# Top-k attention and two feed-forward layers on one core: the steps behind one top-k pair moved up, two weight rows converted at the start

## The chip, the cores and the metric

The program runs on one core of one Trainium2 chip. The metric is the device time of one execution in microseconds (us). The kernel before took 1209.21 us (median of 3 runs, 1208.96 to 1211.28).

## What is computed

The reference, cut to its core:

```python
scores = scale * np.matmul(q, k.transpose(0, 1, 3, 2))      # 4 x 8 heads, 576 x 576, head size 64
kth = np.partition(scores, -top_k, axis=-1)[..., -top_k:-top_k + 1]   # top_k = 32
scores = np.where(scores >= kth, scores, -1000000000.0)
attn = np.exp(scores - np.max(scores, axis=-1, keepdims=True))
attn = attn / (np.sum(attn, axis=-1, keepdims=True) + 1e-09)
x = np.matmul(attn, v)                                      # as 2304 rows of 512
h = np.maximum(x @ w_in, 0.0);  x = h * h @ w_out           # first layer, 512 -> 2048 -> 512
h = x @ w_in;  out = np.maximum(0.01 * h, h) @ w_out        # second layer
```

## The kernel before, in words

**Attention.** 2304 query rows are cut into units (`UNITS`), each unit into four head pairs ("uh" in the code), each of these into tiles of 128 partitions x 576 scores; two neighbouring tiles are a *pair*, and there are 72. For a pair VectorE (DVE) finds the 32 largest of every row: four times MAX8 and three times MATCH_REPLACE8 per tile (L829, L831), 14 instructions, one per slot. The program is written as a list of events by *slot*, 16 slots to a pair. Behind the top-k of pair p (z = 16 p) stand: `shifts` on POOL (L288, L289), `drop` and `expo_sum` on ACT (L295, L299), `recip` on POOL and DVE (L303, L304), the transposes on TensorE and their copies on ACT (`pt_main`, `pt_left`, L313 to L362), the product with V on TensorE (`av`, L397), and `x_out`: a multiplication on DVE (tile `xn`, L428), a copy on ACT (`xh`, L429) and a difference on POOL (`xl`, L432). They were put at z + 14 to z + 34.

**Scores.** Tiles of batches 0 and 1 are scored just ahead of their top-k (tiles `sd`, later `att`, into buffers `s`). Those of batches 2 and 3 are scored early, spread over slots 2 to 245 (`FILL`): TensorE into `sp`, ACT into `stage` (L277), a DMA into DRAM (L280).

**The two layers.** Rows are gathered into blocks (`BLOCKS`, the first has 512 rows). When a block's last `x_out` is emitted, both layers of it start (`moe`): for each of 16 weight rows of a layer 12 matmuls into `h` (L575) and as many into `acc` (L618, L620), cut into quanta that are spread evenly over the slots up to the next block's completion (`rate`). The first block is complete with pair 15. At that slot (`rslot[0]`, 274) the pools of the early scores are closed and those of the layers opened, so `h` also waits for the last `sp` and `stage`.

**Weights.** A weight row comes from DRAM as two tiles `wraw` of 64-bit numbers (L486, 0.5 MB each; four buffers). `w_convert_steps` makes fp32 of each half and splits it: two ACTIVATEs (L509 into `wc`, L510 into a PSUM bank `att`), two SCALAR_TENSOR_TENSORs on DVE (L514, L515), an ACTIVATE (L519) and a POOL difference (L521) into `wi` or `wo`; it is then stored (L529, L530) for later blocks. Row 0 was loaded from slot `rslot[0]` - 80 on and converted at - 28, row 1 at - 14.

**What sets the order.** The Tile framework schedules the recorded instructions on each engine's in-order queue. `tc.high_priority(offset=...)` moves what is recorded inside it that many places forward in its ranking: events have `SOON = 100`, weight conversions `CONVP = 30` beside it.

```python
for fn, a in events.pop(slot, []):
    nr = len(ready)
    with tc.high_priority(offset=SOON):
        fn(*a)
```

Of the kernel before, what the change touches and what calls it, by code (L numbers as in the profile page):

```python
# [31 lines left out]
BLOCKS = [512, 256, 384, 512, 256, 384]  # L32
# [24 lines left out]
DLEAD = 30  # L57
LEAD = 24

SOON = 100  # L60
CONVP = 30

HI_SET = (0, 1, 2, 3, 4, 5, 6, 7, 8, 9, 10, 11, 12, 13, 14, 15)
# [8 lines left out]
def topk_attention_moe_moe2_kernel(  # L72
# [10 lines left out]
    B, NHP, _, _, S = q.shape  # L83
    D = v.shape[-1]
    P = 128
# [37 lines left out]
    uhs = []  # L123
    tiles = []
    for u in units:
        for hp in range(NHP):
            n = u["n"]
            uh = dict(u=u, hp=hp, n=n, b=u["b"], first=(u["t0"] == 0), ti=len(tiles), idx=len(uhs),
                      c0=P * (hp % 2) if n == 64 else 0)
# [14 lines left out]
    def direct(uh):  # L144
        return uh["b"] not in EARLY
# [4 lines left out]
    def split(uh):  # L150
        return uh["u"]["i"] >= NATIVE
# [35 lines left out]

    def at(slot, fn, *a):
        events.setdefault(slot, []).append((fn, a))


    KT = {}
# [299 lines left out]
    def w_convert(i):  # L492
        g = w_convert_steps(i)
        while True:
            with tc.high_priority(offset=CONVP):
                if next(g, 1):
# [150 lines left out]
    def score_slot(ti):  # L647
        return 16 * (ti // 2) - DLEAD + 5 * (ti % 2)
# [5 lines left out]
    for uh in uhs:  # L654
        b, hp, i = uh["b"], uh["hp"], uh.get("di")
        z = score_slot(uh["ti"])
        if uh["first"] and direct(uh):
            st = {"i": i}
            st["n"] = len(order)
            order.append(b)  # L660
            z0 = after(z - 62, ("kraw", st["n"] - KRB), *[("KT", x, hp) for x in range(b)])
            at(z0, load_k, b, hp, st)
            for h in range(2):
                at(z0 + 12 * h + 11, split_k, b, hp, st, h)
            used["kraw", st["n"]] = z0 + 23
            assert z0 + 24 <= z
        if (b, hp) not in vdone or split(uh) and VTB < NHP:
            assert not uh["u"]["i"] < NATIVE <= units[max(x["i"] for x in units if x["b"] == b)]["i"]
            vdone.add((b, hp))
            zv = z + DLEAD + 4  # L670
            if split(uh):
                zv = max(zv, opened)
            at(zv, load_v, uh)
            if split(uh):
                at(zv + 6, split_v, uh, 0)
                at(zv + 9, split_v, uh, 1)
# [55 lines left out]
        done += w  # L732

    pairs = []
    for p in range(NPAIRS):
        pr = dict(t=tiles[2 * p:2 * p + 2], p=p)
        pairs.append(pr)
        z = 16 * p
        for i, t in enumerate(pr["t"]):
            if direct(t["uh"]):  # L740
                at(z - DLEAD + 5 * i, scores, t, 0)
                at(z - DLEAD + 2 + 5 * i, scores, t, 1)
            else:
                at(z - LEAD + i, load_s, t)
            if i == 0:
                at(z + 14, shifts, pr)
            at(z + 14 + i, drop, pr, i)
            at(z + 16 + i, expo_sum, pr, i)
            if split(t["uh"]):
                at(z + 20 + i, norm, pr, i)  # L750
            at(max(z + 20 + 3 * i, z + 21 + i), pt_main, t)
        at(z + 18, recip, pr)
        at(z + 26, pt_left, pr)
    rslot = [None] * len(blocks)

    def rmark(uh, z):
        if uh["hp"] == NHP - 1:
            e = uh["u"]["g0"] + uh["n"]
            for blk in blocks:
                if rslot[blk["idx"]] is None and blk["g0"] + blk["n"] <= e:  # L760
                    rslot[blk["idx"]] = z

    for uh in uhs:
        if split(uh):
            za, z = 16 * (uh["lastA"] // 2) + 30, 16 * (uh["last"] // 2) + 30
            at(za, av_split, uh, 0)
            at(z + 2, av_split, uh, 1)
            z += 4
            at(z, x_out, uh, (0, 1))
            rmark(uh, z)  # L770
            continue
        apart = uh["n"] > P and uh["n"] % P and uh["ti"] % 2 == 0
        for hs in ((0,), (1,)) if apart else ((0, 1),):
            z = 16 * (uh["lastA"] // 2 if hs == (0,) else uh["last"] // 2) + 30
            nq = 2 * len(hs)
            for i in range(nq):
                at(z + i, av, uh, hs, i)
            at(z + nq, x_out, uh, hs)
        z += nq
        if uh["u"]["i"] == NATIVE - 1 and uh["hp"] == NHP - 1:  # L780
            at(z, open_late)
        rmark(uh, z)
# [6 lines left out]
        for _ in w_convert(i):  # L789
            pass  # L790

    at(rslot[0] - 80, w_raw, 0)
    at(rslot[0] - 80, w_raw, 1)
    at(rslot[0] - 28, convert_now, 0)
    at(rslot[0] - 27, w_raw, 2)
    at(rslot[0] - 14, convert_now, 1)
    at(rslot[0] - 13, w_raw, 3)
    at(rslot[0] - 10, w_store, 0)

    active = []  # L800
    credit = 0.0
# [11 lines left out]
    last = max(events)  # L813
    while slot <= last:
        p, i = divmod(slot, 16)
        if slot >= 0 and p < NPAIRS:
            pr = pairs[p]
# [7 lines left out]
            t = pr["t"][x]  # L825
# [9 lines left out]
# [4 lines that stand above are left out]
# [66 lines left out]
```

## Time and profile before

| | us |
|---|---|
| median of 3 runs (1208.96 to 1211.28) | 1209.21 |
| the profiled execution | 1210.15 |
| its span, first to last instruction | 1208.4 |
| TensorE (PE) busy | 1135.8 (94%) |
| VectorE (DVE) busy | 946.5 (78%) |
| ScalarE (ACT) busy | 807.5 (67%) |
| GpSimd (POOL) busy | 682.8 (57%) |

The profile shows one execution; a time in it is counted from the span's first instruction. An instruction's row gives its start, its length, engine, line, operation and `output<-input`; brackets give the idle time of the engine before it and what ended it. Instructions of one engine overlap a little, so what one costs in a full queue is the distance of two starts. PE's busy time is modelled, and a PE that is busy is not always at its peak. The chain of waits is followed back from the last instruction: at each step to what released it, or to the instruction ahead of it on its engine.

### The profile page before, as it was taken

The page shows a single profiled execution, that of the slowest core. Times are in us where ns is not written, and L with a number is a line of the kernel's source. Part 1 is how long each engine was busy: PE and PEld are TensorE (multiplying, and loading weights), DVE is VectorE, ACT ScalarE, POOL GpSimd, SP SyncE. Part 2 cuts the span into 40 slices and gives each one's busy share as a digit, 9 for nine tenths or more (in the row PEclk, how much of TensorE's full clock was granted, in tenths as well). Part 3 has the DMA queues.
Part 4 walks back from the last instruction along what each step waited for, and adds up shares of the span by engine and source line. Part 5 has one row for each costly group of instructions (what it writes and reads, how often), then busy time and mean ns, then how long its engine had stood idle before and what let it go on. Part 6 is the DMA issues. An engine that isn't in the chain of part 4 may idle for free.

```text
span 1208.4 us, 20261 instructions
## 1 busy us (share of the span) xinstructions
PE 1135.8 (94%) x6388; PEld 992.5 (82%) x6388; DVE 946.5 (78%) x1944; ACT 807.5 (67%) x1831; POOL 682.8 (57%) x982
## 2 busy tenths in 40 slices
PE   4988987999889999999999999999999999999998
PEld 3776765887678779988999898888788899999997
DVE  7999899868988999999999999999999930110122
ACT  6988898878998986766656666555666653334322
POOL 7765564877878876556666665555565644004300
PEclk9899897999999999999999999999999999999999
DMA  9765566779989888879988888776676679779974
GB/s 307 255 217 192 192 220 222 267 233 333 342 280 319 305 267 263 296 269 384 355 293 290 298 272 286 221 227 226 201 239 211 199 255 369 253 253 341 356 256 135
DMA packets 110522, 323.25 MB, mean 268 GB/s; under 512 B 17488, under 2 KB 25680, under 8 KB 110416
## 3 DMA queue, kind: packets, MB, share of 16 engines
q1 hardware_dynamic: 107776, 317.24, 77.5%
q10 hardware_dynamic: 2640, 4.72, 1.1%
q8 instruction: 52, 0.85, 0.3%
q14 instruction: 54, 0.44, 0.1%
HBM read 254.54 MB, written 67.37 MB: 266 GB/s over the span
## 4 chain that ended last, share of the span: by engine, by line
PE 71%; ACT 11%; DVE 7%; DMA 6%; issue 2%; POOL 1%; ACTq 0%; SPq 0%; POOLq 0%; DVEq 0%
PE h L575 29%; PE acc L620 14%; PE acc L618 14%; PE att L408 4%; PE att L313 4%; DVE m L829 3%; PE att L397 3%; DVE w L831 3%; DMA wraw<-in_w_dram 2%; DMA sd<-stage 2%; ACT stage L277 1%; ACT e L299 1%; ACT e L295 1%; ACT s L277 1%; PE sp L276 1%
## 5 line engine op out<-in xcount | busy, mean ns | idle before, releaser
L575 PE MATMUL h<-xh,wi 128*128 128x512 f32 (+2 forms) x1280 | 349.9, 345 | 13.4 <-ACT gb L597 4.2
L829 DVE MAX8 m<-w 128x8 f32<-128x576 f32 x432 | 311.9, 748 | 1.1
L575 PEld LDWEIGHTS h<-xh,wi 128*128 128x128 f32 x1280 | 227.5, 191 | 42.6 <-ACT gb L597 5.8
L831 DVE MATCH_REPLACE8 w<-m,w 128x576 f32<-128x576 f32 x288 | 213.5, 744 | 0.8
L575 PE MATMUL h<-xl,wi 128*128 128x512 f32 (+2 forms) x640 | 207.6, 342 | 0.6 <-DVE xl L632 0.6
L601 POOL TENSOR_TENSOR gl<-ga,gh 128x512 fp32r<-128x512 f32 (+2 forms) x160 | 162.7, 1017 | 37.9 <-ACT gh L600 32.1
L618 PE MATMUL acc<-gh,wo 128*128 128x512 f32 (+2 forms) x768 | 156.8, 340 | 0.0
L620 PE MATMUL acc<-wo,gh 128*128 128x512 f32 x576 | 152.5, 399 | 2.9 <-ACT gh L600 2.7
L598 POOL TENSOR_TENSOR ga<-ga,gb 128x512 f32<-128x512 f32 (+2 forms) x80 | 81.4, 1017 | 130.6 <-ACT gb L597 127.3
L618 PEld LDWEIGHTS acc<-gh,wo 128*128 128x128 f32 x768 | 126.5, 189 | 11.0 <-ACT gh L586 0.2
L575 PEld LDWEIGHTS h<-xl,wi 128*128 128x128 f32 x640 | 121.4, 191 | 12.3 <-DVE xl L632 1.1
L295 ACT ACTIVATE e<-s,m 128x576 f32<-128x576 f32 x144 | 111.7, 779 | 18.6 <-DVE m L829 13.4
L620 PEld LDWEIGHTS acc<-wo,gh 128*128 128x128 f32 x576 | 104.3, 189 | 24.1 <-ACT gh L600 5.0
L829 DVE MAX8 m<-s 128x8 f32<-128x576 f32 x144 | 104.1, 748 | 12.5 <-ACT s L277 6.1
L299 ACT ACTIVATE e<-e,nb 128x576 f32<-128x576 f32 x144 | 111.0, 774 | 3.2 <-POOL nb L289 2.8
L587 POOL TENSOR_TENSOR ga<-ga 128x512 f32<-128x512 f32 (+2 forms) x80 | 66.1, 827 | 78.1 <-ACT gh L586 72.8
L831 DVE MATCH_REPLACE8 w<-m,s 128x576 f32<-128x576 f32 x144 | 107.1, 744 | 0.6
L313 PE MATMUL att<-ident,e 128*128 128x128 f32 x576 | 90.8, 281 | 13.7 <-ACT e L299 5.1
L313 PEld LDWEIGHTS att<-ident,e 128*128 128x128 f32 x576 | 70.0, 143 | 27.4 <-ACT e L299 10.1
L308 POOL TENSOR_SCALAR e<-e,rc 128x576 f32<-128x576 f32 x108 | 79.8, 749 | 22.5 <-DVE rc L304 21.1
L585 ACT ACTIVATE ga<-h 128x512 f32<-128x512 f32 (+2 forms) x80 | 39.0, 488 | 77.4 <-PE h L575 71.9
L618 PE MATMUL acc<-gl,wo 128*128 128x512 f32 (+2 forms) x384 | 87.7, 345 | 0.1
(94 smaller groups left out, 2136.7 us busy)
## 6 DMA issues: line engine op xcount, KB each, us to landing
wi<-wd SPq DMA_DIRECT2D x160, 512.0 KB, 5.0
wo<-wd SPq DMA_DIRECT2D x160, 512.0 KB, 5.2
wraw<-in_w_dram SPq DMA_DIRECT2D x64, 512.0 KB, 6.0
sd<-stage SPq DMA_DIRECT2D x72, 288.0 KB, 2.9
s<-sd SPq DMA_DIRECT2D x72, 288.0 KB, 4.6
wd<-wi SPq DMA_DIRECT2D x32, 512.0 KB, 5.4
wd<-wo SPq DMA_DIRECT2D x32, 512.0 KB, 5.9
kraw<-in_k_dram SPq DMA_DIRECT2D x16, 576.0 KB, 5.4
```

Source lines behind the costliest of these rows:

```text
L295: ACT.activation(t["e"], t["s"], AF.Prelu, bias=pr["m8"][:, i, 31:32], scale=-1.0, alpha=0.125 / FAR)
L299: ACT.activation(e, e, AF.Exp, bias=pr["nb"][:, i:i + 1], scale=-FAR, accum_out=pr["sum"][:, i:i + 1])
L308: POOL.tensor_scalar(e, e, pr["rc"][:, i:i + 1], 1.0, op0=OP.mult, op1=OP.mult)
L313: PE.transpose(ps[:, j * P:(j + 1) * P], t["e"][:, j * P:(j + 1) * P], ident)
L575: PE.matmul(h[:, 0:n], lhsT=wi[:, w, c * P:(c + 1) * P], rhs=x[c][y][:, 0:n], start=cnt == 0, stop=cnt == 3 * NK - 1)
L587: POOL.tensor_tensor(a[:, 0:n], a[:, 0:n], a[:, 0:n], op=OP.mult)
L598: POOL.tensor_tensor(a[:, 0:n], a[:, 0:n], b[:, 0:n], op=OP.subtract)
L601: (DVE if j >= GLD else POOL).tensor_tensor(gl[:, 0:n], a[:, 0:n], gh.bitcast(F)[:, 0:n], op=OP.subtract)
L618: PE.matmul(acc[c][:, 0:n], lhsT=wo[:, w, cs], rhs=g[:, 0:n], start=first, stop=last)
L620: PE.matmul(acc[c], lhsT=g[:, cs], rhs=wo[:, w, :], start=first, stop=last)
L829: cur["dve"] = DVE.max(out=m8[:, x, 8 * r:8 * r + 8], in_=t["s"] if r == 0 else t["w"])
L831: cur["dve"] = DVE.match_replace(out=t["w"], in_to_replace=m8[:, x, 8 * r:8 * r + 8], in_values=t["s"] if r == 0 else t["w"], imm_value=NEG)
```

## The change

Three edits go together. The steps behind pair 15's top-k are recorded at z + 13 and z + 14, with a priority of 800 places (`urgent`), and so are the second head's product with V and its `x_out`; for that head pair the two heads are now handled apart, the first at slot 251 and the second at 255. `rslot[0]` becomes 257 instead of 274, so the layers' quanta of the first block are spread over 176 slots instead of 159. Weight rows 0 and 1 are loaded at slots -20 and -19 and converted at -6 and -3, ahead of the first top-k, and rows 2 and 3 are loaded from `rslot[0]` - 60 on.

```diff
+URGENT = 800
...
+    def urgent(fn):
+        def run(*a):
+            with tc.high_priority(offset=URGENT):
+                fn(*a)
+        return run
...
+    first_done = next(uh["last"] // 2 for uh in uhs if uh["hp"] == NHP - 1 and uh["u"]["g0"] + uh["n"] >= BLOCKS[0])
...
+        if p == first_done:
...
+            at(z + 13, urgent(shifts), pr)
+            for i in range(2):
+                at(z + 13, urgent(drop), pr, i)
+                at(z + 13, urgent(expo_sum), pr, i)
+            at(z + 13, urgent(recip), pr)
+            for i in range(2):
+                at(z + 14, urgent(pt_main), pr["t"][i])
+            at(z + 14, urgent(pt_left), pr)
+            continue
...
-        apart = uh["n"] > P and uh["n"] % P and uh["ti"] % 2 == 0
+        tight = uh["last"] // 2 == first_done
+        apart = uh["n"] > P and (uh["n"] % P or tight) and uh["ti"] % 2 == 0
         for hs in ((0,), (1,)) if apart else ((0, 1),):
-            z = 16 * (uh["lastA"] // 2 if hs == (0,) else uh["last"] // 2) + 30
+            near = tight and hs[-1] == 1
+            z = 16 * (uh["lastA"] // 2 if hs == (0,) else uh["last"] // 2) + (15 if near else 27 if tight and apart else 30)
             nq = 2 * len(hs)
             for i in range(nq):
-                at(z + i, av, uh, hs, i)
-            at(z + nq, x_out, uh, hs)
+                at(z + i, urgent(av) if near else av, uh, hs, i)
+            at(z + nq, urgent(x_out) if near else x_out, uh, hs)
...
-    at(rslot[0] - 80, w_raw, 0)
-    at(rslot[0] - 80, w_raw, 1)
-    at(rslot[0] - 28, convert_now, 0)
-    at(rslot[0] - 27, w_raw, 2)
-    at(rslot[0] - 14, convert_now, 1)
-    at(rslot[0] - 13, w_raw, 3)
-    at(rslot[0] - 10, w_store, 0)
+    for i in range(2):
+        at(i - DLEAD + 10, w_raw, i)
+        at(3 * i - 6, convert_now, i)
+        at(rslot[0] - 60, w_raw, i + 2)
+    at(20, w_store, 0)
```

The order in which the built programs' instructions stand shows what the scheduler makes of it. Line numbers of the changed kernel are 7 higher up to L362, L397 becomes L404, L428 L435, L514 and L515 become L521 and L522, L829 and L831 become L851 and L853.

**DVE at the start.** Before; `m8` is the top-k's result, `s0` to `s3` are score buffers:

```order
1 L255 TENSOR_TENSOR q10_78<-qraw_148,q00_77 128x256 x2
2 L238 TENSOR_TENSOR KT_150<-kraw_151,KT_150 64x576 x2
3 L829 MAX m8_217<-s0_101 128x8
4 L831 MATCH_REPLACE w_220<-m8_217,s0_101 128x576
5 L829 MAX m8_217<-s1_102 128x8
6 L829 MAX m8_217<-w_220 128x8
7 L831 MATCH_REPLACE w_221<-m8_217,s1_102 128x576
```

The same place in the changed kernel:

```order
1 L262 TENSOR_TENSOR q10_78<-qraw_148,q00_77 128x256 x2
2 L521 SCALAR_TENSOR_TENSOR wc_223<-att_224,wc_223 128x512
3 L522 SCALAR_TENSOR_TENSOR wc_223<-att_224,wc_223 128x512
4 L245 TENSOR_TENSOR KT_150<-kraw_151,KT_150 64x576 x2
5 L521 SCALAR_TENSOR_TENSOR wc_231<-att_232,wc_231 128x512
6 L851 MAX m8_261<-s0_101 128x8
7 L522 SCALAR_TENSOR_TENSOR wc_231<-att_232,wc_231 128x512
8 L853 MATCH_REPLACE w_264<-m8_261,s0_101 128x576
9 L521 SCALAR_TENSOR_TENSOR wc_245<-att_246,wc_245 128x512
10 L851 MAX m8_261<-w_264 128x8
```

Three instructions of the conversion now stand ahead of the first MAX8, five more in rows 7 to 15; the same eight stood in rows 249 to 274 before.

**DVE between pair 15's last MAX8 and the first block's last `xn`**, in the changed kernel: `m8_2358` is pair 15, `m8_2499` pair 16, `m8_2729` pair 17.

```order
259 L851 MAX m8_2358<-w_2362 128x8
260 L851 MAX m8_2499<-w_2502 128x8
261 L853 MATCH_REPLACE w_2503<-m8_2499,w_2503 128x576
...
268 L853 MATCH_REPLACE w_2502<-m8_2499,w_2502 128x576
269 L435 TENSOR_TENSOR xn_2472<-att_2448,rb_2444 64x256
270 L851 MAX m8_2499<-w_2503 128x8
...
275 L521 SCALAR_TENSOR_TENSOR wc_2528<-att_2529,wc_2528 128x512
...
279 L853 MATCH_REPLACE w_2733<-m8_2729,s5_106 128x576
280 L435 TENSOR_TENSOR xn_2516<-att_2495,rb_2444 64x256
```

Before, pair 15's last MAX8 stands in row 254 and the last `xn` in row 288. In the changed kernel the distance is 21 rows instead of 34. Row 275 is the first on weight row 2 (`wc_2528`), ahead of the last `xn`; before, that was row 290, behind it. Counted from the program's start, the last `xn` has 104 MATCH_REPLACEs, 139 MAXes, 10 SCALAR_TENSOR_TENSORs and one other `xn` of this head pair ahead of it, where there were 108, 145, 8 and none.

**ACT at the start**, in the changed kernel; before, row 2 was followed by the `KT` row at once:

```order
2 L114 ACTIVATE q00_77<-qraw_148 128x256 x2
3 L516 ACTIVATE wc_223<-wraw_191 128x512
4 L517 ACTIVATE att_224<-wraw_191 128x512
5 L114 ACTIVATE KT_150<-kraw_151 128x576 x2
6 L114 ACTIVATE q01_83<-qraw_157 128x256 x2
7 L526 ACTIVATE wi_221<-wc_223 128x512
8 L516 ACTIVATE wc_231<-wraw_193 128x512
9 L517 ACTIVATE att_232<-wraw_193 128x512
10 L284 ACTIVATE s0_101<-sd_179 128x288
11 L284 ACTIVATE s0_101<-sd_172 128x288
```

The eviction of the first scores (`s0`) now stands behind the conversion of the first two `wraw` tiles, and rows 12 to 17 alternate `s1` with the third and fourth.

## Rows read from the trace of the kernel before

**Rows 1.** Busy time by stage: window, length, PE, PEld, DVE, ACT, POOL, clock, DMA

```profile
0.00:204.00 204.00, 160.50 (x852) 128.19 (x853) 188.41 (x402) 174.81 (x461) 129.03 (x226) 0.92 0.70 230
204.00:444.00 240.00, 226.97 (x1109) 184.97 (x1107) 204.35 (x387) 210.59 (x436) 194.50 (x214) 0.99 0.85 292
```

**Rows 2.** Chain of waits by line, from 440 to 960 and from 960 us on

```profile
by line: PE h L575 36.2%; PE acc L620 18.0%; PE acc L618 17.1%; PE att L408 7.7%; PE att L313 6.2%; PE att L326 1.5%; DVE m L829 1.5%; PE att L276 1.3%; DVE w L831 1.3%; DVE xl L632 1.0%; POOL VT L230 0.8%; ACT y L635 0.7%; DMA wo<-wd 0.6%;
...
by line: PE h L575 46.1%; PE acc L620 24.4%; PE acc L618 22.9%; PE att L408 1.7%; ACT y L635 1.3%; PE att L313 1.0%; ACTq L637 0.4%; issue 0.3%; PE att L326 0.2%; ACT ga L585 0.2%; ACTq L635 0.0%
```

**Rows 3.** Timeline of PE where the first layer starts

```profile
203.68 1.43 PE L575 MATMUL h<-xh,wi 128*128 128x512 f32 x5 [0.87 <-ACT xh L429]
204.94 1.07 PE L575 MATMUL h<-xl,wi 128*128 128x512 f32 x4
```

**Rows 4.** Timelines of POOL, DVE and ACT: three steps behind pair 15's top-k

```profile
179.77 0.20 POOL L288 TENSOR_TENSOR nb<-m 128x2 f32<-128x2 f32 x1 [0.42 <-DVE m L829]
...
201.68 0.42 DVE L428 TENSOR_TENSOR xn<-att,rb 128x256 f32<-128x256 f32 x1
...
203.22 0.41 ACT L429 ACTIVATE xh<-xn 128x256 fp32r<-128x256 f32 x1
```

**Rows 5.** Timeline of DVE in a full queue: the distance between starts

```profile
188.87 0.67 DVE L514 SCALAR_TENSOR_TENSOR wc<-att,wc 128x512 uint32<-128x512 uint32 x1
189.45 0.08 DVE L831 MATCH_VALUE_LOAD w<-m,w 128x8 f32 x1
...
198.90 0.08 DVE L831 MATCH_VALUE_LOAD w<-m,w 128x8 f32 x1
...
199.63 1.41 DVE L829 MAX8 m<-w 128x8 f32<-128x576 f32 x2
```

**Rows 6.** Timeline of the start, and the busy time and DMA rate (GB/s, last) there

```profile
1.45 0.58 SPq L201 DMA_DIRECT2D kraw<-in_k_dram  x1
...
5.61 1.25 ACT L113 ACTIVATE KT<-kraw 128x576 fp32r<-128x576 f32 x2 [0.90 <-DMA kraw<-in_k_dram]
...
9.01 0.76 DVE L829 MAX8 m<-s 128x8 f32<-128x576 f32 x1 [1.25 <-ACT s L277]
...
12.11 1.30 POOL L115 TENSOR_SCALAR KTa<-kraw 128x576 fp32r<-128x576 f32 x2
...
0.00:10.00 10.00, 2.60 (x8) 1.96 (x8) 3.15 (x7) 5.09 (x10) 5.48 (x31) 1.00 0.77 261
...
20.00:30.00 10.00, 6.17 (x37) 4.68 (x35) 9.98 (x22) 9.27 (x24) 6.99 (x12) 1.00 1.03 382
```

**Rows 7.** What DVE waited for from 0 to 204 us: total, times, longest

```profile
DVE m L829 <- ACT e L295: 5.6, 4, 2.8
DVE q L255 <- ACT q L113: 4.4, 1, 4.4
```

**Rows 8.** The early scores' matmuls (min/median/max ns, first and last start), and the chain from 48 to 176 us

```profile
L276 PE MATMUL sp<-KTa,q x320: 288/295/609, 17.3 to 179.4; 128*128 128x288 f32 x160
...
by line: PE att L397 22.4%; DMA sd<-stage 14.3%; ACT stage L277 13.3%; PE sp L276 9.6%; ACT s L277 6.1%; issue 5.9%; PE sd L276 4.9%; ACT e L299 4.4%; PE att L313 4.1%; ACT PT L321 3.5%; ACT e L295 2.5%; ACT q L113 2.4%; ACT KT L113 1.8%; P
```

**Rows 9.** Chain from 204 to 444 us, and what DVE waited for there

```profile
by line: PE h L575 20.0%; DMA wraw<-in_w_dram 11.4%; PE acc L618 9.8%; PE acc L620 7.8%; issue 4.5%; DMA vraw<-in_v_dram 4.4%; ACT att L510 4.0%; ACT e L299 3.3%; ACT e L295 3.0%; ACT wc L509 2.9%; PE att L397 2.5%; PE att L313 2.1%; ACT gh
...
DVE wc L514 <- ACT att L510: 19.4, 14, 4.9
```

**Rows 10.** Timelines: an idle ACT queue, and DVE's first step on weight row 2

```profile
200.76 0.41 ACT L277 ACTIVATE s<-att 128x288 f32<-128x288 f32 x1 [2.77 <-PE att L276]
...
202.74 0.68 DVE L514 SCALAR_TENSOR_TENSOR wc<-att,wc 128x512 uint32<-128x512 uint32 x1
```

**Rows 11.** PE at low and at full clock: a window, and two stretches of `av`

```profile
180.00:200.00 20.00, 13.28 (x40) 9.19 (x41) 19.04 (x41) 16.38 (x37) 9.42 (x12) 0.57 0.75 264
...
193.79 6.67 PE L397 MATMUL att<-PT,VN 128*128 128x256 f32 x18
...
167.09 2.62 PE L397 MATMUL att<-PT,VN 128*128 128x256 f32 x10 [1.42 <-ACT PT L321]
```

More of the change, by code (lines that the diff above doesn't have):

```diff
@@ L738, in topk_attention_moe_moe2_kernel @@
         z = 16 * p
+        if p == first_done:
+            assert all(direct(t["uh"]) and not split(t["uh"]) for t in pr["t"])
+            for i, t in enumerate(pr["t"]):
+                at(z - DLEAD + 5 * i, scores, t, 0)
+                at(z - DLEAD + 2 + 5 * i, scores, t, 1)
+            at(z + 13, urgent(shifts), pr)
[7 more added lines that the diff above has]
+            continue
         for i, t in enumerate(pr["t"]):
```

## The prediction

> **What bounds the kernel now.** I read the busy time by stage first, then the chain of waits for each stage, then timelines where two stages meet. The busy table [rows 1] cuts the span in two at 204 us: the reader is to see that PE is idle for 204 - 160.5 = 43.5 us before the layers start, and for 240 - 227.0 = 13 us between 204 and 444 us. From 440 us on the chain [rows 2] is nearly all PE: `h`, `acc` and the attention's own matmuls follow each other, and DVE has under 4% of it up to 960 us and next to none behind. So what is worth anything is PE time lost before 444 us; behind that the end moves with it, one for one.
>
> The first block's layers start in earnest at 203.68 us, when the last `xh` lets five matmuls go, and the first on `xl` follows at 204.94 [rows 3]. What they wait for begins at 179.77, where POOL starts on the finished top-k of pair 15; the last `xn` comes at 201.68 and its `xh` at 203.22 [rows 4]. That is 21.9 us from top-k to `xn`, for a dozen instructions none of which takes 1 us: they stand behind others in in-order queues. The change aims there.
>
> **The change, part by part.** *The queue ahead of the last `xn`.* In a full DVE queue a MATCH_REPLACE8 with its load takes 199.63 - 198.90 = 0.73 us, a MAX8 1.41 / 2 = 0.70, a step of the conversion 189.45 - 188.87 = 0.58 [rows 5]. By the order, the last `xn` now has 4 MATCH_REPLACEs and 6 MAXes fewer ahead of it (2.9 + 4.2 us) and two conversion steps (1.2) and one `xn` (0.4) more: 5.5 us less. It is not the whole 21.9: 16 top-k instructions of the next two pairs, two conversion steps and another `xn` still stand between pair 15 and that `xn`, some 13 us, and the scheduler put them there because the chain through ACT, PE and back takes about as long. The other moved steps are the same instructions on the same engines; splitting one `x_out` in two adds one instruction of 0.42 us or so on each of DVE, ACT and POOL [rows 4], which lies beside other work.
>
> *The two weight rows at the start.* Moved are 8 DVE steps, 12 ACTIVATEs, 4 POOL differences, 4 loads and 4 stores. DVE's and ACT's share is already in the count above, since these stood ahead of the last `xn` before as well; they cost nothing unless DVE waits for them. The four loads do cost: each is 128 x 1024 x 4 bytes = 0.52 MB, the first now ahead of the first K (0.59 MB) on SP's queue, the others directly behind it and one q tile (0.26 MB). K was issued at 1.45 us and ACT had it at 5.61 [rows 6]. ACT now evicts the first scores only behind the second weight tile, which has 1.3 MB more ahead of it and in it than K had. At the 261 GB/s of the first 10 us or the 382 of the third 10 us [rows 6] that is 5.0 or 3.4 us, so it lands at 9.0 to 10.6; with two conversions at 0.62 (as K's halves) and two evictions at 0.41 [rows 6, 10] behind it, 2.0 us, the first MAX8 starts at 11.0 to 12.6 instead of 9.01. DVE fills 1.8 us of that with three conversion steps, so its idle time grows by 0.2 to 1.8, and perhaps by 1 more at the third and fourth tile. I take 1.3.
>
> The Trainium skill (DMA: Bandwidth & Descriptors, "Anatomy of one DMA") puts the moving of data at bytes / 436e9 s, by which the added 1.3 MB would take 3.0 us and the sum below would be about 1.5 us better. The trace's windows at 261 and 382 GB/s do not reach that rate, and they decide.
>
> *Sum for the layers' start.* DVE's other waits (5.6 us in four places behind ACT, rest at the start [rows 7]) I leave as they are. The last `xn`: 201.68 - 5.5 + 1.3 = 197.5, 4.2 earlier, and with it the first `h` on the last head pair, at 199.5. PE has then done 6 score matmuls and 4 transposes fewer; at half of 295 ns [rows 8] each, as they overlap, that is 1.5 us to be done later. PE idle time saved: 2.7 us.
>
> *The early scores* could be the next thing late: `h` waits for the last of them. Their K is loaded behind 2.1 MB more (5.5 to 8.0 us at the two rates), and two POOL differences now stand ahead of its split, priced at 1.30 us each by the longest POOL row near [rows 6]. So they start 8 to 11 us later than 17.3, at 25 to 28, and with the 162 us they took before [rows 8] the last comes at 188 to 190. That is covered by some 9 us; without the cover each us costs one.
>
> *The weights behind the start.* Between 204 and 444 us the chain leaves PE often: the loads of `wraw` have 11.4% of it, and DVE waited 19.4 us for conversions [rows 9]. DVE's first step on weight row 2 came 0.9 us ahead of the full `h` (202.74 against 203.68 [rows 3, 10]); now it stands five rows ahead of the last `xn`, 3.3 us by [rows 5], so 5.3 us ahead of `h`. This lead of 4.4 us is used once. If only PE binds it is worth 0, if the weights bind all of it. As the chain shows both, I take 2.5.
>
> *Sum.* 2.7 + 2.5 = 5.2 us: 1210.15 - 5.2 = 1205.0 for the profiled execution, which stood 0.94 above the median of the runs; for the median 1209.21 - 5.2 = **1204.0 us**. The forecast's own range is 1201 to 1206.5.
>
> **Rivals.** *DVE takes it back, no change (0.21).* The ten top-k instructions that no longer precede the last `xn` are still to be done, 5.5 us of DVE net, now between 204 and 444 us. DVE is idle for 240 - 204.4 = 35.6 us there [rows 1], which speaks against it; but 19.4 of that are waits inside its in-order queue [rows 9], which more work doesn't fill by itself. If none is filled, the block ends 5.5 later after a start 4.2 earlier: 1210.5.
>
> *The first stage is late as a whole, slower (0.13).* Place: the score evictions on ACT behind loads of weights, and the early scores' K. From 48 to 176 us the chain is made of `av`, `stage`, its DMA and `sp`, and DVE doesn't lead it [rows 8]; then the pace isn't DVE's, and the 8 to 11 us by which the early scores start late shift all of it, pair 15 too. The moved steps win 21.9 - 13 = 8.9 us at the most if every one goes at once; if half of it, `h` starts 9.5 - 4.5 = 5 us later. It decides from 204.6 us on for the first of the five matmuls (203.68, less the 1.5 us of PE work left over, plus 2.4); at 207 the time is 1209.2 + 3.3 + 1.5 = 1214. Against it: DVE is 188.4 of 204 us busy [rows 1].
>
> The Trainium skill (TensorE: Matmul & The Clock Gate, "Architectural detail") says that ACT and DVE are strict FIFO; by that rule a conversion that waits for its load holds every eviction behind it, which is this rival's mechanism. The trace agrees as far as it shows: ACT sat idle for 2.77 us at 200.76 behind one eviction [rows 10].
>
> *More than forecast (0.18).* PE ran at a granted clock of 0.57 from 180 to 200 us, mostly at its lower level of 1.2 GHz, after standing idle, and 18 matmuls of `av` took 6.67 us where 10 took 2.62 at full clock [rows 11]: 6.67 - 18 x 0.262 = 2.0 us on pair 15's path. With early scores now next to these steps PE need not fall to the lower level. If that, half of DVE's 5.6 us of waits [rows 7] and the whole 4.4 of the weights come: 2.7 + 2.0 + 2.8 + 4.4 = 11.9, so 1197.5 to 1201.
>
> *The change doesn't do what it says (0.02):* the order shows it does, though 16 top-k instructions remain between; the time would be 1209.
>
> **How the numbers follow.** Forecast 0.46, the others as given. A measurement of this kernel tells about 0.2% from no change, 2.4 us, so "faster" is below 1206.8. It holds the forecast save 0.02 and all of "more": 0.62. Slower, above 1211.6: the late stage, and 0.02 of the DVE case with a late start: 0.15. The rest is 0.23. The range reaches from 1198, which leaves out a small part of "more", to 1211.5, which leaves out the slower case.
>
> **What would show it.** Right: the first MAX8 at 11.0 to 12.6 us, the last `xn` near 197.5, the five matmuls of `h` near 199.5, the last `sp` near 190 and ahead of it, `h` and `acc` of the first block done some 5 us before 444, and the chain all PE behind that. Wrong: `h` held by `stage` or `sp` instead of `xh`; a first `h` near 199 with the first block's end unmoved, DVE busier between (the first rival); or PE stalls behind 444 us of more than the few it has, by the new order of its queue, which I can't price and take for 2 us either way.

## The result: slower by half a per cent, and the profile after

The changed kernel takes 1216.49 us (median of 17 runs, 1211.61 to 1225.25), the kernel before 1210.40 in the same job (17 runs, 1207.81 to 1212.95): a ratio of 1.0052, 95% interval 1.0039 to 1.0065. The forecast was 1204.0, faster. The profiled execution took 1212.28 us (span 1210.5), one of the fastest of its kernel, so its trace shows some 2 of the 6 us.

The busy time by stage of the changed kernel, and 740 to 760 us, where the difference lies; columns as in [rows 1]:

```profile
0.00:204.00 204.00, 158.58 (x847) 127.69 (x848) 186.46 (x397) 173.85 (x459) 131.00 (x227) 0.96 0.70 231
204.00:444.00 240.00, 226.49 (x1110) 182.78 (x1109) 203.65 (x388) 210.94 (x437) 192.28 (x212) 1.00 0.85 289
740.00:760.00 20.00, 14.34 (x60) 10.91 (x59) 19.77 (x42) 11.94 (x25) 4.68 (x11) 0.74 0.62 194
```

The last window in the kernel before:

```profile
740.00:760.00 20.00, 17.99 (x91) 14.45 (x90) 19.76 (x42) 13.48 (x29) 9.50 (x15) 1.00 0.81 271
```

The first two rows hardly differ from [rows 1]. In the third PE did 60 matmuls instead of 91, at a granted clock of 0.74 instead of 1.00, while DVE was busy for 19.8 of 20 us in both. Timelines of DVE, POOL, ACT and PE of the changed kernel, up to where the first layer starts (answering to [rows 3, 4, 6]); the POOL row is its first step on pair 15's top-k:

```profile
12.91 0.76 DVE L851 MAX8 m<-s 128x8 f32<-128x576 f32 x1
...
187.30 0.19 POOL L295 TENSOR_TENSOR nb<-m 128x2 f32<-128x2 f32 x1
...
198.84 0.43 DVE L435 TENSOR_TENSOR xn<-att,rb 64x256 f32<-64x256 f32 x1
...
202.25 0.41 ACT L436 ACTIVATE xh<-xn 64x256 fp32r<-64x256 f32 x1
...
199.65 0.96 PE L582 MATMUL h<-xh,wi 128*128 128x512 f32 x3 [0.84 <-ACT stage L284]
...
202.72 1.43 PE L582 MATMUL h<-xh,wi 128*128 128x512 f32 x5
203.99 1.09 PE L582 MATMUL h<-xl,wi 128*128 128x512 f32 x4
```

The layers start 1 us earlier, not 4. Still, PE gets ahead: the second layer's first outputs `y` (L642, before L635) of the first three blocks come at 445.3, 577.8 and 743.5 us, before at 445.9, 587.0 and 746.9. Part of the 9 us in the middle is order: by 578 us PE had done 2909 matmuls against 2889, and 20 matmuls at the 0.23 us between two of 512 columns are some 5 us. With the fourth block, the 512 rows that pair 51 completes, the lead is gone: 976.2 against 969.4. That is not the whole balance either: at these two times PE had done 4973 matmuls against 4955, and the rest took 234.3 us against 239.0. (The code counts blocks from 0; where my expectations say "third block" in connection with pair 51, this one is meant.) PE's timeline there, before:

```profile
742.03 1.64 PE L620 MATMUL acc<-wo,gh 128*128 128x512 f32 x6
...
747.12 1.11 PE L408 MATMUL att<-PTs,VT 128*128 128x256 f32 x8
748.88 1.38 PE L313 MATMUL att<-ident,e 128*128 128x128 f32 x8 [0.65 <-POOL e L308]
750.10 0.38 PE L326 MATMUL att<-ident,e 128*64 128x128 f32 x2
751.09 1.43 PE L575 MATMUL h<-xh,wi 128*128 128x512 f32 x5 [0.60 <-ACT xh L429]
```

and after:

```profile
743.47 0.38 PE L333 MATMUL att<-ident,e 128*64 128x128 f32 x2
744.78 0.36 PE L415 MATMUL att<-PTs,VT 128*128 128x256 f32 x1 [0.92 <-DVE PTs L326]
746.01 1.76 PE L415 MATMUL att<-PTs,VT 128*128 128x256 f32 x8 [0.88 <-DVE PTs L326]
750.94 1.12 PE L320 MATMUL att<-ident,e 128*128 128x128 f32 x4 [3.17 <-POOL e L315]
751.71 2.48 PE L582 MATMUL h<-xh,wi 128*128 128x512 f32 x5
```

Before, PE still had matmuls of the third block to put between (`acc` at 742.03) and lost little over 1 us to waits. After, it had used them up; it stood idle for 5.0 us (0.92 + 0.88 + 3.17) behind steps that follow DVE's top-k, fell to the lower clock (from 750 to 755 us the granted clock is 0.50), and the five `h` took 2.48 instead of 1.43 us. These five start 0.6 us later than before, and DVE's last step for that block, `xf`, 1.4 us later (750.7 against 749.3). The chain of waits from 440 to 960 us, by line, answers to the first row of [rows 2]:

```profile
by line: PE h L582 33.7%; PE acc L625 19.2%; PE acc L627 13.8%; PE att L415 7.5%; PE att L320 6.0%; DVE m L851 4.6%; DVE w L853 3.7%; PE att L283 1.4%; PE att L333 1.4%; ACT e L302 1.1%; issue 1.1%; ACT e L306 1.0%; ACT PTs L325 0.9%; DMA w
```

DVE's top-k (`m`, `w`) has 8.3% of it, where it had 2.8%. So DVE, not PE, says when the fourth block starts. And DVE came there no earlier: its last MAX8 of pair 51, found by its place in the built order, ends at 732.1 us, before at 731.3. From 204 to 444 us, while the first block ran, its idle time ahead of weight conversions had grown:

```profile
DVE wc L521 <- ACT att L517: 24.7, 16, 4.2
DVE m L851 <- ACT s L284: 5.4, 4, 2.4
```

24.7 us against 19.4 in [rows 9]; in all it was busy there for 203.7 us, before for 204.4. The longest of these waits, in the timelines of ACT, PE and DVE after, and a shorter one:

```profile
250.57 0.60 ACT L592 ACTIVATE ga<-h 128x512 f32<-128x512 f32 x1 [0.94 <-PE h L582]
...
251.77 0.41 ACT L284 ACTIVATE s<-att 128x288 f32<-128x288 f32 x1 [0.46 <-PE att L283]
252.08 0.62 ACT L593 ACTIVATE gh<-ga 128x512 fp32r<-128x512 f32 x1
252.60 0.63 ACT L517 ACTIVATE att<-wraw 128x512 f32<-128x512 f32 x1
...
253.90 0.41 ACT L284 ACTIVATE s<-att 128x288 f32<-128x288 f32 x1
...
253.44 0.43 PE L283 MATMUL att<-KT,q 128*128 128x288 f32 x2
...
253.26 0.69 DVE L521 SCALAR_TENSOR_TENSOR wc<-att,wc 128x512 uint32<-128x512 uint32 x1 [4.17 <-ACT att L517]
...
254.60 0.75 DVE L851 MAX8 m<-s 128x8 f32<-128x576 f32 x1
...
297.87 0.69 DVE L521 SCALAR_TENSOR_TENSOR wc<-att,wc 128x512 uint32<-128x512 uint32 x1 [1.39 <-ACT att L517]
298.47 0.08 DVE L853 MATCH_VALUE_LOAD w<-m,w 128x8 f32 x1
298.54 0.74 DVE L853 MATCH_REPLACE8 w<-m,w 128x576 f32<-128x576 f32 x1
```

In the first, DVE stands for 4.2 us ahead of a conversion whose input comes from ACT; on ACT that step stands behind `ga` and a score eviction, which waited 0.94 and 0.46 us for PE. But the MAX8 behind the conversion would hardly have been earlier without it: by the built order, it reads scores whose second half ACT evicted at 253.90 to 254.31, and PE had computed that half at 253.44, behind matmuls of the layers. The conversion cost it 0.3 us; the rest is scores that came late. In the second, the MATCH_REPLACE8 reads only what DVE had written itself, and lost the 1.4 us to the conversion. Over all conversions from 204 to 444 us whose wait the trace shows (26.2 us, with waits for POOL; before 20.7), the inputs that the next instruction takes from ACT or DVE were there for 7.9 us at the most (before 3.2). So a wait put down to a conversion is for the larger part a wait for scores as well.

### The profile page after: what moved, and what is told of

It is laid out like the page before. It is cut to its first block, busy times and chain, and to the rows that moved or that the text cites. A ratio compares the mean times of both kernels' runs of the same rounds, so it can differ in the third digit from the quotient of the medians.

```text
span 1210.5 us, 20253 instructions
## 1 busy us (share of the span) xinstructions
PE 1133.5 (94%) x6388; PEld 989.8 (82%) x6388; DVE 945.9 (78%) x1945; ACT 806.9 (67%) x1832; POOL 684.1 (57%) x983
## 4 chain that ended last, share of the span: by engine, by line
PE 70%; ACT 11%; DVE 8%; DMA 6%; issue 3%; POOL 2%; SPq 0%; ACTq 0%; POOLq 0%
PE h L582 28%; PE acc L625 15%; PE acc L627 13%; DVE m L851 4%; PE att L415 4%; PE att L320 4%; PE att L404 3%; DVE w L853 3%; DMA wraw<-in_w_dram 2%; DMA sd<-stage 2%; ACT e L306 2%; PE sp L283 2%; ACT stage L284 2%; ACT e L302 1%; ACT s L284 1%
## 5 line engine op out<-in xcount | busy, mean ns | idle before, releaser
L851 DVE MAX8 m<-w 128x8 f32<-128x576 f32 x432 | 313.4, 748 | 1.6
L582 PEld LDWEIGHTS h<-xh,wi 128*128 128x128 f32 x1280 | 224.8, 189 | 38.8 <-ACT gb L604 5.4
L853 DVE MATCH_REPLACE8 w<-m,w 128x576 f32<-128x576 f32 x288 | 213.6, 743 | 0.6
L851 DVE MAX8 m<-s 128x8 f32<-128x576 f32 x144 | 104.5, 748 | 9.6 <-ACT s L284 5.4
L853 DVE MATCH_REPLACE8 w<-m,s 128x576 f32<-128x576 f32 x144 | 107.0, 743 | 0.4
L283 PE MATMUL sp<-KTa,q 128*128 128x288 f32 x320 | 67.4, 337 | 22.5 <-ACT stage L284 13.2
L607 ACT ACTIVATE gh<-ga 128x384 fp32r<-128x384 f32 (+2 forms) x112 | 58.6, 523 | 42.1 <-POOL ga L605 32.1
```

What stands on the lines that cost most here:

```text
L283: PE.matmul(ps[:, 0:HALF], lhsT=l, rhs=r, start=i == 0, stop=i == len(mm) - 1)
L582: PE.matmul(h[:, 0:n], lhsT=wi[:, w, c * P:(c + 1) * P], rhs=x[c][y][:, 0:n], start=cnt == 0, stop=cnt == 3 * NK - 1)
L851: cur["dve"] = DVE.max(out=m8[:, x, 8 * r:8 * r + 8], in_=t["s"] if r == 0 else t["w"])
L853: cur["dve"] = DVE.match_replace(out=t["w"], in_to_replace=m8[:, x, 8 * r:8 * r + 8], in_values=t["s"] if r == 0 else t["w"], imm_value=NEG)
```

## The experiments

Eighteen more kernels ran; two of them, e4 and (as it turned out) e8, are the changed kernel again. Each median has the kernel before of its own job beside it; the ratio is of the two.

**1. Which part of the change loses (e1 to e4).** e1 is the changed kernel with the weights' old schedule (counted from its new start of the layers), e2 the kernel before with the new one alone, e3 the changed kernel with rows 0 and 1 loaded and converted later, e4 the changed kernel again. The edit of e1; e2 makes the opposite one in the kernel before:

```diff
-    for i in range(2):
-        at(i - DLEAD + 10, w_raw, i)
-        at(3 * i - 6, convert_now, i)
-        at(rslot[0] - 60, w_raw, i + 2)
-    at(20, w_store, 0)
+    at(rslot[0] - 80, w_raw, 0)
...
+    at(rslot[0] - 28, convert_now, 0)
...
+    at(rslot[0] - 14, convert_now, 1)
...
+    at(rslot[0] - 10, w_store, 0)
```

> The urgent steps and the two heads apart, with the weight rows loaded and converted where they were before (relative to the new first slot). Theory A (DVE's finish sets the end; what DVE idles ahead of 970 us is lost, and the early conversion adds it at the start): first MAX8 at 9.0 us as before, DVE idle up to 204 us about 15 us, time 1206 to 1210.5, not above before. Theory B (the moved steps disturb the queues and lose the time; the conversion at the start is harmless): 1214 to 1217, as the whole change.

> The early loads and conversions alone, the steps behind pair 15 as before. Theory A: first MAX8 at about 12.9 us, as in the whole change, DVE idle up to 204 us 2 us or more above before, time 1212 to 1217. Theory B: 1208.5 to 1211, as before.

e3 (`w_raw` of both at slot 10, `convert_now` at 30 and 50, `w_store` at 56):

> The whole change, but rows 0 and 1 loaded from slot 10 and converted at slots 30 and 50, behind the first two pairs instead of ahead of them. Theory A: first MAX8 at 9.0 us, time 1206 to 1210.5. Theory B: 1214 to 1217, as the whole change.

> The changed kernel itself, for a profile of a second execution beside the first, which was one of its fastest (1212.28 of a median of 1216.49). Theory A: a slower execution shows more DVE idle time ahead of 970 us and PE waiting for DVE's results behind 740 us; 1212 to 1219. Theory B: the added time stands in PE or ACT waits between 180 and 444 us.

| | median us | ratio to before | 95% |
|---|---|---|---|
| e1 steps only | 1215.83 | 1.0064 | 1.0042 to 1.0086 |
| e2 weights only | 1206.67 | 0.9974 | 0.9960 to 0.9987 |
| e3 weights later | 1217.31 | 1.0061 | 1.0045 to 1.0077 |
| e4 after, again | 1216.54 | 1.0062 | 1.0046 to 1.0078 |

Theory A, which blamed the early weights, fell: they alone gain 0.26%, 2 us more than theory B had. What is left of the change, the moved steps with the earlier start of the quanta, loses it all.

**2. Is it DVE at pair 51, and which of the steps (e5 to e8).** e5 and e6 take work off DVE shortly before pair 51 by searching 64 of the 576 columns in three pairs, so their output is another:

```diff
+SHORT = (44, 45, 46)
...
+            n = 64 if p in SHORT else S
...
-                cur["dve"] = DVE.max(out=m8[:, x, 8 * r:8 * r + 8], in_=t["s"] if r == 0 else t["w"])
+                cur["dve"] = DVE.max(out=m8[:, x, 8 * r:8 * r + 8], in_=t["s"] if r == 0 else t["w"][:, 0:n])
...
```

> The kernel before, with the top-k of pairs 44 to 46 searching 64 of the 576 columns after its first round (so the thresholds of these pairs, and their rows of the output, are others): some 20 us less work for DVE ahead of the third block's last pair. Theory D (the third block can't start before DVE has finished pair 51's top-k; what PE wins ahead of that is lost there, and PE's idle time brings the low clock with it): PE reaches that point 2 us ahead of DVE here, so the gain is small, 1204 to 1209. Theory Q (the loss lies in the order of PE's own queue or in the spread of the quanta, wherever DVE is): nothing changes, 1207 to 1212.

> The changed kernel with the same 64 columns in pairs 44 to 46 (thresholds of these pairs and their rows are others). Theory D: PE was 3 to 8 us ahead when it met DVE, so this gains more than the kernel before did from the same cut: 1199 to 1206, below the relieved kernel before by 1 to 6 us, and from 740 to 760 us the trace shows PE busy at full clock. Theory Q: still about 6 us above the relieved kernel before, 1212 to 1217.

Measured: e5 1203.97 (ratio 0.9960, 0.9946 to 0.9974), e6 1207.51 (0.9979, 0.9964 to 0.9994). The cut gained 6 us before and 9 after; the gap shrank from 6 to 3.5 us but did not close or turn, as theory D had it, so both theories were half right. PE has no wait left at pair 51, whose top-k now ends at 711.5 us in e5 and 713.4 in e6; e6:

```profile
710.00:740.00 30.00, 30.00 (x173) 27.40 (x172) 29.25 (x63) 19.76 (x45) 18.37 (x28) 1.00 0.78 267
740.00:760.00 20.00, 20.00 (x100) 16.82 (x99) 19.08 (x40) 12.27 (x27) 9.17 (x13) 1.00 0.93 321
```

e7 holds the quanta back, e8 takes the priority away (`URGENT = 0`):

```diff
+    rslot[0] += 17
...
-                active.extend(moe(*ph) for ph in groups[blk["idx"]])
...
+                if blk["idx"] == 0:
+                    at(rslot[0], start, blk)
+                else:
+                    start(blk)
```

> The changed kernel, in which the urgent steps and the early weights stay but the first block's quanta start at slot 274 and are spread over 159 slots, as before. If the earlier start and the longer spread of the quanta lose the time (Q, and D in so far as PE then no longer runs ahead): 1205 to 1210, as with the early weights alone (1206.7). If the urgent steps themselves lose it, by what they displace on DVE, ACT and POOL (theory P): 1213 to 1217.

> The changed kernel with URGENT = 0: the steps keep their early slots, the heads stay apart, the quanta start at slot 257, but nothing jumps 800 places forward. Theory P: 1205 to 1210. Theories D and Q: as the changed kernel, 1214 to 1217.

e7: 1209.15 (1.0002, 0.9989 to 1.0014); the loss is gone, though the steps are still moved. In its build PE's last 4157 of 6268 matmuls stand in the order of before, while in the changed kernel the order differs up to the last 1260. That by itself is no loss: the order differs as far in e2, with the early weights alone, which gains, and in every other build but e7's it agrees for 1261 at the most. So each comparison here, e5 with e6 and e12 with e13 too, is also one of two orders. e8: 1214.79 (1.0047, 1.0032 to 1.0063). Built, its instructions stand in the same order as the changed kernel's on all five engines, so the priority of 800 places moves nothing at all and e8 is a third measurement of the same program. The loss goes with where the quanta start; the edit also changes how they are spread, when the layers' buffers are opened and the order that follows, and no run takes these apart.

**3. Other starts (e9 to e11).** The edit of e7 with 8 and 26 in place of 17 (slots 265 and 283), and 283 in the kernel with only the early weights.

> The changed kernel with the first block's quanta started at slot 265 (257 in the changed kernel, 274 before). Theory M (a matter of degree: the earlier the quanta stand among the attention's matmuls, the later DVE gets its scores and the more PE has used up when it meets DVE at pair 51): between the two, 1211 to 1215. Theory O (only the old order of the queues behind the start was good; any other start sorts them anew and loses): 1213 to 1218. Theory R (each new order falls as it may, without a trend): anywhere from 1203 to 1217.

> The same with the quanta started at slot 283, nine slots later than before and spread over 150. Theory M: at or below the 1209 of the start at slot 274, 1205 to 1209.5. Theory O: 1213 to 1218. Theory R: anywhere from 1203 to 1217.

> The kernel with only the early weights (1206.7), with the quanta started at slot 283 instead of 274. Theory M: faster again, 1202 to 1206. Theory O: its own new order was good by luck, and another one loses: 1208 to 1216. Theory R: anywhere from 1203 to 1217.

| start of the quanta | 257 (e4) | 265 (e9) | 274 (e7) | 283 (e10) | weights only, 274 (e2) | weights only, 283 (e11) |
|---|---|---|---|---|---|---|
| median us | 1216.54 | 1221.92 | 1209.15 | 1208.14 | 1206.67 | 1209.03 |
| ratio | 1.0062 | 1.0115 | 1.0002 | 0.9998 | 0.9974 | 1.0001 |
| DVE busy, 204 to 444 us | 202.6 | 200.8 | 205.8 | 206.8 | 209.3 | 208.9 |

Both starts ahead of slot 274 lose and both others don't, so theory O (only the old order is good) fell. M (a matter of degree) missed e9 by 7 us and e11 by 3, and R (no trend) missed e9 by 5: there is a tendency, and several us that each new order of the queues deals out. What goes with the time in this table is how much DVE got done while the first block ran.

**4. Taking DVE out of the conversions (e12, e13).** The same edit in both kernels:

```diff
-                v = bank()
                 ACT.activation(b, lo, AF.Copy, scale=L_SCALE, bias=L_BIAS)
-                ACT.activation(v, hi.bitcast(F), AF.Copy, scale=H_SCALE)
+                ACT.activation(b.bitcast(F), hi.bitcast(F), AF.Copy, scale=H_SCALE)
...
-                with behind("dve"):
-                    DVE.scalar_tensor_tensor(b, vu, 3, b, op0=OP.logical_shift_left, op1=OP.bitwise_or)
-                DVE.scalar_tensor_tensor(b, vu, 0x80000000, b, op0=OP.bitwise_and, op1=OP.bitwise_or)
...
```

> The kernel before, with the weights' conversion left without its two DVE steps (the weights are then only the upper half of each number, by ACT alone, and the output is another): 128 DVE steps of 0.58 to 0.67 us and all waits for them are gone in the first block. Theory W (the loss of the changed kernel is DVE's waiting for conversions in the first block, paid at pair 51): DVE is some 90 us ahead, the wall at pair 51 is gone, 1185 to 1200. Theory V (the order of PE's own queue): 1190 to 1205.

> The changed kernel with the same left out. Theory W: no slower than the kernel before without these steps, from 5 us faster to 1 us slower, since its layers start earlier and nothing takes it back. Theory V: still 4 us or more slower than that one.

e12 1195.77 us (0.9875, 0.9855 to 0.9895), e13 1191.62 (0.9847, 0.9824 to 0.9870). Without these steps the changed kernel is the faster one, by 4.2 us (their ranges, 1194.56 to 1200.70 and 1191.42 to 1193.29, don't meet). Theory W's forecast for this pair held, V's failed. In e13 pair 51's top-k ends at 707.1 us and the block's last `xf` starts at 729.1; between them PE still waits 1.5 us, at full clock:

```profile
710.00:730.00 20.00, 18.55 (x105) 16.40 (x104) 19.77 (x43) 12.50 (x28) 11.76 (x16) 1.00 0.77 256
```

The edit takes the waits for conversions away, but also 128 steps of work off DVE. It shows that with less work on DVE the change no longer loses, not that these waits were the cause; and 4.2 us is no more than two orders of the queues can differ by.

**5. Is spacing the conversions a cure (e14 to e18).** All work stays; a row's two halves are interleaved, so that two quanta lie between ACT's step and DVE's:

```diff
+        halves = []
         for raw, w in zip(wraw.pop(i), w2):
...
+            halves.append((b, v, w))
             yield 0
+        for b, v, w in halves:
+            vu = v.bitcast(U)
...
```

> The kernel before, with the conversion of a weight row's two halves interleaved, so that two quanta instead of one lie between ACT's step and DVE's. Theory W: the 19.4 us that DVE waits for conversions between 204 and 444 us fall to 10 or less, DVE is 5 to 9 us earlier at pair 51, and half of that is kept: 1204 to 1208. Theory V: no change, 1207 to 1212. Against both: the two halves now hold two of the three PSUM banks that the attention shares, which could make its scores late.

> The changed kernel with the same interleaving. Theory W: the 24.7 us of waits fall to 12 or less, DVE is earlier at pair 51 by 6 to 12 us, and most of the loss comes back: 1206 to 1211. Theory V: 1213 to 1218.

> Early weights alone (1206.7) with the spaced conversions. Theory W1 (the spacing cures DVE's waits): DVE waits less than its 16.6 us for conversions from 204 to 444 us, has done more than 791 instructions by 444 us, and the time is 1201 to 1206. Theory R (each new order of the queues falls as it may, the spacing is just another draw): anywhere from 1204 to 1221, and where DVE has done fewer than 785 instructions by 444 us, above 1212.

> The changed kernel with the quanta started at slot 283 (1208.1) and the spaced conversions. Theory W1: less than 16.3 us of waits for conversions, 1202 to 1207. Theory R: anywhere from 1204 to 1221, by the same count of DVE's instructions (792 without the spacing).

> Early weights alone with the quanta started at slot 283 (1209.0) and the spaced conversions. Theory W1: 1202 to 1208. Theory R: anywhere from 1204 to 1221, by the same count (798 without the spacing).

| spaced | median us | ratio | 95% | median without | DVE busy 204 to 444 us | without |
|---|---|---|---|---|---|---|
| e14 before | 1221.47 | 1.0090 | 1.0066 to 1.0114 | 1209.62 | 199.0 | 204.4 |
| e15 after | 1207.28 | 0.9974 | 0.9959 to 0.9989 | 1216.54 | 206.5 | 203.7 |
| e16 weights only | 1216.13 | 1.0062 | 1.0044 to 1.0080 | 1206.67 | 204.9 | 209.3 |
| e17 start 283 | 1217.97 | 1.0062 | 1.0042 to 1.0081 | 1208.14 | 201.8 | 206.8 |
| e18 weights only, start 283 | 1210.85 | 1.0014 | 0.9997 to 1.0030 | 1209.03 | 205.9 | 208.9 |

The changed kernel became faster by 9 us; three others became slower and e18 by no more than can be told. W's forecast for e14 failed with them, and in e15 the waits for conversions fell to 17.9 us only, not to 12. What DVE waited for from 204 to 444 us in e17:

```profile
DVE m L859 <- ACT s L284: 17.6, 9, 7.4
DVE wc L523 <- ACT att L517: 9.6, 9, 1.8
```

In e10, the same start without spacing:

```profile
DVE wc L521 <- ACT att L517: 16.3, 16, 2.4
DVE m L857 <- ACT s L284: 10.0, 7, 3.7
```

The waits for conversions fall (16.3 to 9.6 us) and those for score evictions rise (10.0 to 17.6); the sum stays (26.3 and 27.2). That is what late scores behind both kinds of wait would give. In e14 the first go from 19.4 to 17.6, the second from 4.9 to 15.2, so there the sum grew by 8.5. That the two banks held by the halves make the scores late fits, but no run changed the number of banks alone. Theory W1 fell: in all five pairs the time goes against how busy DVE is in this stretch, whatever it waits for.

Over sixteen profiles (the two kernels and all runs that leave nothing out) DVE's instructions done by 444 us go against the median with a correlation of -0.80: the seven programs below 1211.5 us had done 788 to 798, the nine above 775 to 786, e1 (789) excepted. One execution's count is rough: after, e4 and e8 are the same program and had 784, 783 and 776.

The end of DVE's last MAX8 of pair 51 sorts the same sixteen without an exception: 723.6 to 731.3 us in the seven, 731.7 to 737.8 in the nine (correlation with the median 0.84). PE's idle time there (from 5 us ahead of that end to 25 us behind it) does not sort them (0.33). e2, the fastest, has it at 727.6 us, and PE stands idle behind it as long and falls as low as in the changed kernel:

```profile
740.00:760.00 20.00, 13.23 (x48) 10.19 (x49) 19.77 (x42) 11.14 (x25) 6.25 (x11) 0.74 0.57 171
```

So it is how far DVE has come that goes with the time; that PE stands idle shows only that it was ahead. These are single executions, and 731.3 (before) and 731.7 (e4) are close.

e2 and e15 beat both kernels, by 0.26% against the kernel before. No version stood clear of these.

## Why the prediction was wrong, point by point

- *First MAX8 at 11.0 to 12.6:* 12.91. Nearly; the third conversion step on DVE waited 1.4 us just ahead of it. These first 12.91 us moved 281 GB/s, between the two rates that I used. The row of the Trainium skill that I set beside them, DMA: Bandwidth & Descriptors, "Anatomy of one DMA", is written for transfers that GpSimd issues; these loads are issued by SP.
- *Last `xn` at 197.5:* 198.84, so 2.8 us earlier than before instead of 4.2. DVE's work ahead of it fell by 4.8 us (186.1 to 181.3) where I had 5.5, and its idle time grew by 1.9 (15.6 to 17.5) where I had 1.3. The moved steps did what they should: from POOL's start on pair 15's top-k to that `xn` it now takes 11.5 us (187.30 to 198.84) where it took 21.9 [rows 4]; but that top-k itself came 7.5 us later.
- *First of the five `h` at 199.5:* 202.72. I gave `xn` to `xh` the 1.5 us of before. It took 3.4: from 198.9 to 202.2 ACT had two `stage`, two `s`, two exponentials `e` and a weight conversion to do ahead of it, where before it had been idle for 2.77 us [rows 10].
- *Last `sp` at 188 to 190, covered:* 198.0. They started at 27.4, in the range given, but then took 171 us instead of 162. The three `h` at 199.65 waited for `stage`; `xh` came later still, so this cost nothing, but there was no cover left. The rival of the late first stage had its place right (the loads on SP, the evictions on ACT), and pair 15 did come 7.5 us later, near the 8 to 11 it had; but the moved steps won 10.4 us, more than its 8.9 at the most, and the delay is not what loses: e2 has it too (first MAX8 at 11.9, last `sp` at 202.3) and is faster than before.
- *The weights' lead, 2.5 us:* the first block ended at 445.3 against 445.9. In this trace there is no such lead; the chain from 204 to 444 us gives `wraw` 11.7%, after 11.4% in [rows 9].
- *The end moves with PE one for one behind 444 us:* this is the step that failed. I read it from the chain, in which DVE had 2.8% [rows 2]. But from 444 to 960 us DVE is busy for 98% of the time, before and after, as PE is, and PE already waited 1.3 us for steps behind it at pair 51: a chain shows what ended last, not how close the second was. PE's lead at 578 us was worth nothing beyond the small slack at pair 51, since DVE ended that pair's top-k 0.8 us later than before; and standing idle there cost the full clock as well. With less work on DVE the same change gains 4.2 us (e13 against e12), near the 5.2 of my sum; as new orders scatter by more than that, the nearness may be luck.
- *The rival "DVE takes it back", 0.21, no change:* the right engine, and the only one of the rivals that pointed there. I weighed its work (5.5 us) against 35.6 us of idle time, as if that could be filled. It was not: DVE was busy there for no longer than before (203.7 us against 204.4), as much of its idle time is spent on scores that are not there yet. Nor did I ask where it is paid. So it ended slower, not level.
- *The rival "more than forecast", 0.18:* its premise came true, the granted clock from 180 to 200 us was 0.91 instead of 0.57 [rows 11], and nothing of it was left at the end.
- *PE's new order, "2 us either way":* a term I could not price. The stalls came (5.0 us at pair 51 against 1.3), but e2 has as much idle time there and gains. e7, e9 to e11 and e14 to e18, whose edits all bring new orders, lie between 2 us below and 13 above the kernel before of their jobs.

The rule that I had set beside the trace (the Trainium skill, TensorE: Matmul & The Clock Gate, "Architectural detail": ACT and DVE are strict FIFO) agrees with the trace at 297.87 us above, where the MATCH_REPLACE8 stands behind the conversion for 1.4 us. I had applied it to the first 10 us alone.

What stays open: what keeps DVE waiting from 204 to 444 us when the layers start earlier (busy for 203.7 us, with the early weights alone for 209.3), since its waits there mix conversions with late scores; how the 6 us divide between that and the low clock, since the profiled executions of the changed kernel are among its fast ones; and why a start at slot 265 is worse than one at 257.

## What to carry to other kernels

An engine that is 98% busy beside the one on the chain is a second limit: find the place where the first must wait for the second, and count an earlier start only up to there. When a wait stands ahead of one instruction, ask whether the one behind it was ready: here a wait for a conversion often hid one for scores, and spacing the conversions moved it from one name to the other. And before crediting one edit, build it apart and compare the whole order on every engine: here the priority did nothing, the early weights alone gained, the earlier start lost, and nearly every edit re-sorted the queues to the end of the scores.

## What the runs showed that was not expected

In one execution PE's clock fell while PE was busy, and DVE paid for it. e8 is the changed kernel's program once more; its windows around the wait shown above:

```profile
245.00:250.00 5.00, 5.00 (x22) 4.29 (x21) 3.06 (x6) 2.45 (x5) 3.67 (x6) 0.59 0.56 160
250.00:255.00 5.00, 5.00 (x18) 3.98 (x18) 0.00 (x0) 1.02 (x3) 1.60 (x2) 0.73 0.81 292
```

and rows of its timelines of PE, ACT and DVE:

```profile
242.00 5.51 PE L404 MATMUL att<-PT,VN 128*128 128x64 f32 x36
...
249.31 0.63 PE L582 MATMUL h<-xh,wi 128*128 128x512 f32 x1
249.74 0.63 PE L582 MATMUL h<-xl,wi 128*128 128x512 f32 x1
...
253.84 0.60 ACT L592 ACTIVATE ga<-h 128x512 f32<-128x512 f32 x1 [3.57 <-PE h L582]
...
256.53 0.69 DVE L521 SCALAR_TENSOR_TENSOR wc<-att,wc 128x512 uint32<-128x512 uint32 x1 [6.79 <-ACT att L517]
```

From 242 us PE did 36 products with V of 64 columns each, without a gap, and was then at its lower level (1.2 GHz) for part of the next 10 us; in the changed kernel's own profile the same stretch stayed at 1.00. The `h` start 0.43 us apart instead of 0.23, ACT's `ga` waits 3.57 instead of 0.94 us, and DVE 6.79 instead of 4.17: it loses 2.6 us more, where it is the engine that counts. By the Trainium skill (TensorE: Matmul & The Clock Gate, "Wait — 56ns, not 53.3ns?") matmuls of 512 columns start 426.7 ns apart at 1.2 GHz; the 0.43 us agree.

The same clock goes with the scatter of one program: over the 17 runs of the changed kernel the mean granted clock (0.978 to 0.988) and the time (1211.61 to 1225.25 us) have a correlation of -0.79. Why one execution of a program falls there and another doesn't, no run shows.
